# A hand-ordered RWKV-7 + SwiGLU kernel: the same 5742 steps in another order, with SyncE's transfers taken to land later

## The chip, the cores and the metric

The kernel runs on one core of a Trainium2 chip. The core has five engines that work at the same time, each through its own queue in order: TensorE (PE in the profile; PEld is its weight load), VectorE (DVE), ScalarE (ACT), GpSimd (POOL) and SyncE (SP), which here does nothing but start transfers. The metric is the device time of one execution in microseconds, of which several are timed; the median counts. A separate execution is profiled; it has a time of its own, and its span runs from the first to the last instruction.

## The reference, cut to what matters

```python
# r, k, v, w, a, b: (4, 8, 768, 40) float32, batch x heads x tokens x channels
for t in range(S):                                        # 768 tokens, one after the other
    y[:, :, t] = einsum('bhd,bhde->bhe', r_t, state)      # read the 40x40 state of each head
    Sa = einsum('bhde,bhe->bhd', state, a_t)
    state = state * w_t - outer(Sa, b_t) + outer(v_t, k_t)
x = y.transpose(0, 2, 1, 3).reshape(3072, 320)            # heads side by side
xn = x / sqrt(mean(x * x) + 1e-6) * rms_g
out = (silu(xn @ w_gate) * (xn @ w_val)) @ w_out          # 320 -> 1536 -> 320; inputs float64
```

There are 32 independent recurrences (4 batches, 8 heads), each over 768 tokens, and behind them a feed-forward block on 3072 tokens. The feed-forward inputs come as float64 and are made float32 on the chip.

## The kernel before, in words

Tokens are worked on in 24 chunks of 32. Within a chunk the recurrence is written as matrix products, and the part in which each token depends on the tokens before it becomes a unit triangular 32x32 matrix per recurrence, which has to be inverted. For every chunk `c` there are four pieces of program:

- `front(c)` loads the inputs w, a, k, b and v, turns them on PE (`turn`, L498), and builds decayed products over five levels (1, 2, 4, 8, 16 tokens). At each level PE makes 16 small products (`gram`, L495, written `ps<-A,KE`), DVE puts them under a mask into the tile `LT`, and ACT copies others into `KN`. When the last level is in `LT`, four transfers write it to DRAM (`sB<-LT`, L735) and four read it back in another layout into `M` (`M<-sB`, L742).
- `inverse(c)` is 31 pairs of DVE operations (`tmp`, `Yi`, L453) on `M`. Its result goes to DRAM by four transfers (`sY<-Yi`, L766) and comes back by four (`LT<-sY`, L768). The first four chunks use `early_inverse`, which inverts halves and joins them with two PE products (`ps<-M,LT` and `ps<-M`).
- `main(c)` uses the inverse: PE products `state` (`ps<-ST,aP`) and `lower` (`ps<-VU,LT`), an ACT scale `Xs`, the second `lower` (`ps<-Xs,LT`), which needs the inverse back in `LT`, four ACT copies into `VU`, then PE's `update` of the state and a `turn` of `VU`, an ACT copy `vut`, the `score` products, the five `level` products (`ps<-As,KN`), DVE sums into `y`, a `turn4` of `y`, the scaling by the root mean square, and a `turn3` into `xg`. Every second chunk it loads `rn` (r, two transfers of 160 KB).
- `feed(g)`, for two chunks together, is the feed-forward block: per pair of 128-wide slices PE does `h64`, `h` (`ps<-xg,w`) and `out` (`po<-w,hT`), ACT the silu (`sg`), DVE the product (`hT`); at the end four transfers write the result (`out_dram<-o`). `narrow` makes the float64 weights float32, 24 times, between the first chunks.

Chunks overlap: `front(c + 2)` and `inverse(c + 2)` run while `main(c)` does. The PE work of `feed` fills the gaps of the recurrences; it is the filler in this program.

The order is written out. `Plan` only records the 5742 steps with what each reads and writes. `ORDER`, a table of numbers, then says in which order they are issued: each number is a step's distance from the oldest step not yet issued. Each engine's queue is what ORDER leaves for that engine. A "-" in the table issues a filler matmul on the identity (L1010, `po<-ident`, 28 of them), which has no use but to keep PE busy. `PAIRS`, a second table, gives for each PSUM room which of three pairs of PSUM banks it takes (`ps0` to `ps2`); a room is free when its last reader has been issued and has run. All transfers but the first ones and the weights' and inputs' loads on POOL go through SP's queue, one behind the other: `sB`, `M`, `sY`, `LT`, `rn` and `out_dram`. A transfer that has to wait for its data holds up all behind it in that queue.

Of the kernel before, what the change touches and what calls it, by code (L numbers as in the profile page):

```python
# [33 lines left out]
363 362 58 54 55 60 59 56 6 5 391 44 46 28 133 4 39 7 8 40 72 53 10 196 364 367 9 368 68 57 365 193 27 11 13 366 185  # L34
188 184 74 73 69 75 373 12 14 15 369 388 380 70 189 16 17 18 66 183 71 81 80 372 79 84 389 83 42 - - 82 187 93 91 88 76
90 182 78 89 92 20 41 195 34 262 35 85 94 186 321 65 77 102 98 99 103 64 100 87 399 201 43 203 86 101 104 108 109 263
202 477 473 398 95 97 110 476 472 114 105 198 470 475 107 113 112 96 115 197 390 474 118 106 116 199 129 126 117 119
130 111 212 125 222 232 200 120 124 123 - 242 121 211 131 204 134 210 132 208 209 205 - 220 206 213 214 219 207 489 381
471 218 217 223 63 127 128 221 215 824 823 228 227 51 229 233 224 231 67 225 230 819 820 226 491 490 240 237 241 29 320
238 194 30 371 234 216 236 243 239 135 62 61 136 137 138 139 140 141 142 248 143 486 - - 244 235 144 145 247 146 147  # L40
488 382 259 246 148 149 258 249 150 245 151 152 153 154 155 156 36 21 370 254 253 487 260 255 0 156 157 158 159 160 161
251 162 163 835 491 1006 821 1002 338 1007 18 391 392 492 836 496 165 166 37 164 167 249 498 495 837 500 260 497 499
493 121 494 506 310 - 504 505 508 168 501 256 394 509 510 519 507 515 502 311 255 384 321 511 382 373 263 514 518 376
817 512 517 516 520 503 377 264 265 525 521 513 176 172 174 170 177 816 323 374 44 178 169 173 171 175 179 523 375 250
47 31 30 266 267 268 269 524 270 21 530 46 957 526 191 820 528 529 385 522 180 378 383 399 531 534 545 393 312 - 36 313
324 407 32 405 315 537 271 272 532 956 386 395 314 316 325 535 416 533 - 317 408 415 322 326 329 549 49 318 546 330 331
336 400 402 527 273 274 275 276 396 277 278 279 538 280 281 282 283 284 540 541 285 286 287 288 289 290 333 335 403 547
401 339 417 404 332 337 334 342 344 838 2 539 1 291 423 406 548 409 340 190 189 341 420 292 345 421 542 543 544 484 550
551 832 294 426 412 552 553 834 293 410 554 346 347 413 481 425 424 434 411 414 427 536 844 418 295 - 343 348 349 833
# [5 lines left out]
468 580 879 958 615 614 621 887 886 582 0 263 92 - - 261 93 267 259 517 525 602 266 603 604 0 647 538 290 94 316 267 95  # L55
# [10 lines left out]
765 770 79 0 221 572 14 0 381 382 16 761 570 359 - 77 576 - 383 281 17 579 0 370 566 752 106 750 0 0 427 63 0 203 204  # L66
205 213 366 564 367 562 565 559 570 563 558 63 59 207 746 102 104 211 427 60 368 569 288 429 1 3 0 62 759 564 367 368 0
367 759 569 571 368 570 369 580 370 576 208 202 205 758 564 371 259 57 563 260 0 371 567 2 0 371 - 59 208 60 204 202
259 0 207 0 0 569 368 206 207 61 996 274 277 62 369 575 370 371 372 373 374 375 376 420 422 421 424 584 561 423 275 256
0 0 375 376 377 378 379 380 381 382 577 569 570 578 55 0 55 254 0 0 - 380 381 382 383 568 577 384 420 422 423 421 0 0  # L70
559 574 561 529 266 578 0 575 559 584 423 582 55 382 428 426 51 425 583 383 - 578 568 384 385 386 581 387 429 388 389
52 595 570 390 594 424 56 0 524 390 426 568 0 578 577 390 1 0 983 0 2 - 425 427 416 987 986 0 581 0 414 0 384 385 587
# [970 lines left out]
```

## Time and profile before

| | us |
|---|---|
| median of 3 executions | 931.58 (930.19 to 933.2) |
| profiled execution, its own time | 934.37 |
| its span | 932.6 |
| PE busy in the span | 875.7 (94%) |
| DVE, ACT, POOL busy | 723.2, 521.9, 294.9 |
| mean granted TensorE clock by the profile | 0.991 |

A row of a group of instructions gives the line, engine, operation, names (written<-read), sizes, how many, then busy time and mean duration of one in nanoseconds, then the time the engine stood idle just before them and who ended it. A row of the timeline has start and duration, and in brackets the idle time before and its releaser. A row of waits names who waited for whom, with total time, number and longest. The row of a window has its length and then for each engine busy time and count, the granted clock of TensorE and the DMA engines' share.

### The profile page before, as it was taken

The page shows a single profiled execution, that of the slowest core. Times are in us where ns is not written, and L with a number is a line of the kernel's source. Part 1 is how long each engine was busy: PE and PEld are TensorE (multiplying, and loading weights), DVE is VectorE, ACT ScalarE, POOL GpSimd, SP SyncE. Part 2 cuts the span into 40 slices and gives each one's busy share as a digit, 9 for nine tenths or more (in the row PEclk, how much of TensorE's full clock was granted, in tenths as well). Part 3 has the DMA queues.
Part 4 walks back from the last instruction along what each step waited for, and adds up shares of the span by engine and source line. Part 5 has one row for each costly group of instructions (what it writes and reads, how often), then busy time and mean ns, then how long its engine had stood idle before and what let it go on. Part 6 is the DMA issues. An engine that isn't in the chain of part 4 may idle for free.

```text
span 932.6 us, 50195 instructions
## 1 busy us (share of the span) xinstructions
PE 875.7 (94%) x22072; PEld 703.2 (75%) x22072; DVE 723.2 (78%) x2702; ACT 521.9 (56%) x1144; POOL 294.9 (32%) x515
## 2 busy tenths in 40 slices
PE   4776898899999999999999999999999999999998
PEld 4665776677777788777777887887787777878776
DVE  5887778878878888978888888888888887864511
ACT  5887877674555566565555655655545454432211
POOL 8576546404221323432221333412503320200000
PEclk9999999899999999999999999999999999999999
DMA  9653546223242243333323223413414222021000
GB/s 162 104 119 84 126 98 153 73 69 67 55 87 49 46 86 73 71 59 60 70 39 74 64 54 75 89 35 71 88 21 85 61 41 62 11 60 28 3 15 15
DMA packets 146363, 63.01 MB, mean 68 GB/s; under 512 B 128800, under 2 KB 138080, under 8 KB 146144
## 3 DMA queue, kind: packets, MB, share of 16 engines
q1 hardware_dynamic: 125664, 29.46, 17.1%
q0 software_dynamic: 18368, 30.01, 15.1%
q8 instruction: 173, 2.83, 1.3%
q10 hardware_dynamic: 2112, 0.33, 0.3%
q14 instruction: 46, 0.38, 0.1%
HBM read 49.15 MB, written 10.09 MB: 64 GB/s over the span
## 4 chain that ended last, share of the span: by engine, by line
PE 72%; DMA 9%; DVE 6%; ACT 6%; issue 3%; SPq 2%; POOL 1%; DVEq 0%; POOLq 0%; ACTq 0%
PE ps L495 50%; PE po L495 14%; PE ps L498 7%; SPq L492 2%; DMA M<-sB 2%; DMA w<-in_moe_w_out_dram 1%; DMA LT<-sY 1%; DMA w<-in_moe_w_gate_dram 1%; DVE tmp L453 1%; DVE y L453 1%; DMA sY<-Yi 1%; ACT VU L476 1%; ACT KE L476 1%; DVE Yi L453 1%; DMA sY<-M 1%
## 5 line engine op out<-in xcount | busy, mean ns | idle before, releaser
L495 PE MATMUL ps<-xg,w 128*128 128x256 f32 (+1 forms) x1728 | 354.2, 393 | 1.2 <-DVE Yi L453 0.5
L495 PEld LDWEIGHTS ps<-xg,w 128*128 128x128 f32 (+1 forms) x1728 | 263.7, 191 | 49.1 <-issue 12.4
L495 PE MATMUL po<-w,hT 128*128 128x320 f32 x576 | 179.0, 449 | 0.0
L492 POOL DMA_DIRECT2D VU<-in_v_dram x184 | 102.4, 560 | 172.7 <-PE ps L495 78.1
L453 DVE TENSOR_TENSOR tmp<-Yi,M 128x60 f32<-128x60 f32 (+24 forms) x620 | 129.3, 209 | 20.5 <-DMA M<-sB 6.1
L453 DVE TENSOR_TENSOR Yi<-Yi,tmp 128x60 f32<-128x60 f32 (+24 forms) x620 | 129.7, 210 | 13.8
L473 ACT ACTIVATE sg<-ps 128x256 f32<-128x256 f32 x144 | 52.6, 384 | 150.6 <-PE ps L495 143.1
L495 PEld LDWEIGHTS po<-w,hT 128*128 128x128 f32 x576 | 106.0, 192 | 37.4 <-issue 1.9
L476 ACT COPY KE<-K 128x512 f32<-128x512 f32 x168 | 110.6, 662 | 26.2 <-DVE K L453 18.2
L453 DVE TENSOR_TENSOR hT<-ps,sg 128x256 f32<-128x256 f32 x144 | 58.3, 420 | 68.7 <-ACT sg L473 57.4
L453 DVE TENSOR_TENSOR K<-K,T 128x256 f32<-128x256 f32 x240 | 98.9, 421 | 10.2 <-ACT KE L476 8.8
L495 PE MATMUL ps<-A,KE 40*64 40x72 f32 x3840 | 95.0, 247 | 9.0 <-ACT KE L476 1.7
L495 PEld LDWEIGHTS ps<-A,KE 40*64 40x64 f32 x3840 | 79.2, 149 | 28.9 <-issue 9.3
L476 ACT COPY KN<-ps 128x320 f32<-128x320 f32 x144 | 67.4, 471 | 59.1 <-PE ps L495 28.5
L453 DVE COPY_PREDICATED LT<-msk,ps 128x256 f32<-128x256 uint32 x120 | 65.9, 550 | 19.5 <-PE ps L495 10.2
L482 POOL TENSOR_TENSOR ss<-ss,mhalf 128x1 f32<-128x1 f32 x24 | 15.4, 641 | 194.2 <-DVE ss L453 179.2
L453 DVE TENSOR_TENSOR y<-y,ps 128x256 f32<-128x256 f32 x119 | 49.9, 419 | 11.0 <-PE ps L495 7.9
L453 DVE TENSOR_TENSOR A<-A,T 128x128 f32<-128x128 f32 (+1 forms) x168 | 55.8, 335 | 1.5 <-ACT A L476 0.4
L495 PEld LDWEIGHTS ps<-As,KN 64*40 64x40 f32 x3840 | 45.1, 123 | 12.7 <-issue 4.4
L495 PE MATMUL ps<-As,KN 64*40 64x32 f32 x3840 | 50.3, 204 | 3.1 <-DVE y L453 1.6
L476 ACT COPY VU<-ps 32x320 f32<-32x320 f32 x96 | 40.0, 417 | 15.5 <-PE ps L495 14.2
L492 POOL DMA_DIRECT2D wan<-in_w_dram x44 | 29.1, 661 | 57.4 <-PE ps L498 57.1
(121 smaller groups left out, 1250.2 us busy)
## 6 DMA issues: line engine op xcount, KB each, us to landing
M<-sB SPq DMA_DIRECT2D x80, 128.0 KB, 3.4
rn<-in_r_dram SPq DMA_DIRECT2D x24, 160.0 KB, 4.6
out_dram<-o SPq DMA_DIRECT2D x48, 80.0 KB, 2.3
VU<-in_v_dram POOLq DMA_DIRECT2D x184, 20.0 KB, 2.6
kbn<-in_b_dram POOLq DMA_DIRECT2D x44, 80.0 KB, 3.4
kbn<-in_k_dram POOLq DMA_DIRECT2D x44, 80.0 KB, 3.3
wan<-in_w_dram POOLq DMA_DIRECT2D x44, 80.0 KB, 3.1
wan<-in_a_dram POOLq DMA_DIRECT2D x44, 80.0 KB, 3.3
```

Source lines behind the costliest of these rows:

```text
L453: plan.add("DVE", kind, lambda at: fn(at(o), *m(at)), [o], aps(*args))
L473: plan.add("ACT", "act", lambda at: nc.scalar.activation(at(o), at(a), f, **kw), [o] + aps(acc), [a])
L476: plan.add("ACT", "copy", lambda at: nc.scalar.copy(at(o), at(a)), [o], [a])
L482: plan.add("POOL", "tt", lambda at: nc.gpsimd.tensor_tensor(o, a, b, op), [o], [a, b])
L492: plan.add(by, "dma", lambda at: queue.dma_start(out=o, in_=i), [o], [i])
L495: return o, lhsT, rhs, lambda at: nc.tensor.matmul(at(o), lhsT, rhs, start=start, stop=stop, skip_group_check=True)
L498: return o, i, ident, lambda at: nc.tensor.transpose(at(o), i, ident)
```

## The change: another order

The operations are the same: the same 5742 steps with the same operands, and 28 filler matmuls. What differs is the two tables. ORDER was found anew by a planner that takes each transfer begun by SyncE to land later than its median; with it the pairs of PSUM banks and the places of the fillers were found anew.

```diff
 ORDER = """
-363 362 58 54 55 60 59 56 6 5 391 44 46 28 133 4 39 7 8 40 72 53 10 196 364 367 9 368 68 57 365 193 27 11 13 366 185
+5 4 6 8 7 9 10 11 12 13 14 15 16 17 18 27 363 373 391 362 39 40 54 59 60 55 28 56 381 364 133 194 42 380 72 73 74 58
...
 PAIRS = """
-20404040232242442445224024020000004244422202002424404224422422440012040400242420024244400242220004220404040400022442020
+20404020014242442423002400424420042022200020222004424004402200042010224404422002204040200424222420044442420204204002024
...
```

The engines' queues are alike in a few stretches: PE's order is the same from the `turn4` of chunk 1 to the middle of `feed(0)`, again for 25 steps in chunk 8, and for the last 144 of its steps, from chunk 20's end on. Elsewhere two of five PE steps have the same neighbour as before.

The first place is SP's queue at the inverse of chunk 11. `sY_176` is the DRAM buffer through which the inverse (`Yi`) goes back into `LT_104`; `rn` is the load of r, `out_dram` a piece of the output. Before:

```order
L492 DMA sY_176<-Yi_138 256x1x32
L492 DMA rn_97<-in_r_dram 64x16x40
L492 DMA sY_176<-Yi_138 256x1x32 x3
L492 DMA LT_104<-sY_176 32x8x32
L492 DMA out_dram<-o_170 32x2x320
L492 DMA LT_104<-sY_176 32x8x32 x3
L492 DMA rn_97<-in_r_dram 64x16x40
```

Now:

```order
L492 DMA M_135<-sB_173 32x1024 x2
L492 DMA sY_176<-Yi_138 256x1x32 x4
L492 DMA LT_104<-sY_176 32x8x32 x4
L492 DMA rn_97<-in_r_dram 64x16x40
L492 DMA out_dram<-o_170 32x2x320
```

The load of r and the piece of output stood between the transfers of the inverse, and now stand behind them.

The second place is PE's queue around the `turn4` of chunk 3 (`ident,y_147`). `As,KN` are the last three `level` products of that chunk, which DVE adds into `y_147`; `xg,w` is a filler from `feed(0)`. Before:

```order
L498 MATMUL ps_63<-ident,wan_95 104x64 x16
L495 MATMUL ps_64<-As_145,KN_0_105 40x32 x16
L495 MATMUL ps_64<-As_145,KN_0_108 40x32 x16
L495 MATMUL ps_64<-As_145,KN_0_111 40x32 x16
L495 MATMUL ps_65<-xg_152,w_164 128x256 x2
L495 MATMUL ps_65<-xg_152,w_165 128x256 x2
L495 MATMUL ps_65<-xg_152,w_164 128x256 x4
L495 MATMUL ps_64<-A_131,KE 64x72 x16
L498 MATMUL ps_63<-ident,y_147 128x40 x8
```

Now:

```order
L495 MATMUL ps_64<-As_145,KN_0_111 40x32 x16
L498 MATMUL ps_65<-ident,wan_95 104x64 x16
L495 MATMUL ps_64<-As_145,KN_0_108 40x32 x16
L495 MATMUL ps_64<-As_145,KN_0_105 40x32 x16
L495 MATMUL ps_63<-A_131,KE 64x72 x16
L498 MATMUL ps_64<-ident,y_147 128x40 x8
L495 MATMUL ps_65<-xg_152,w_164 128x256 x2
```

The feed-forward products that stood between the last level product and the turn now stand behind the turn.

The third place is the start of POOL's queue, which loads the first weights (`w_162`) that ACT makes float32 first. Before:

```order
L492 DMA w_162<-in_moe_w_out_dram 128x448
L509 ISA
L509 AFFINE_SELECT ident<-ident 128x128
L492 DMA w_162<-in_moe_w_gate_dram 128x2x256
L548 IOTA vut_91 128x32
```

Now:

```order
L548 IOTA vut_91 128x32
L488 MEMSET wan_95 128x16x24
L492 DMA w_162<-in_moe_w_out_dram 128x448
L492 DMA w_163<-in_moe_w_val_dram 64x256
L492 DMA w_165<-in_moe_w_val_dram 64x256
L492 DMA w_162<-in_moe_w_gate_dram 128x2x256
```

The load of the gate weights was POOL's second transfer and is now its fourth. On SP the first load of r (160 KB) has moved from the fifteenth transfer to the fifth, among the first inputs.

More of the change, by code (lines that the diff above doesn't have):

```diff
@@ L33 @@
 ORDER = """
-363 362 58 54 55 60 59 56 6 5 391 44 46 28 133 4 39 7 8 40 72 53 10 196 364 367 9 368 68 57 365 193 27 11 13 366 185
[L35 to L48, printed above, removed]
@@ L69 @@
[L69 to L72, printed above, removed]
[31 rows of a table removed]
+5 4 6 8 7 9 10 11 12 13 14 15 16 17 18 27 363 373 391 362 39 40 54 59 60 55 28 56 381 364 133 194 42 380 72 73 74 58
@@ new lines @@
+367 53 57 20 34 46 69 75 - 372 41 19 35 - 368 70 71 193 80 79 32 83 76 320 82 81 84 88 89 93 92 90 78 94 91 77 85 62
+184 189 188 185 201 187 95 100 87 365 47 99 49 101 98 102 476 190 262 103 86 202 104 109 108 203 110 105 113 112 96 114
+115 36 97 106 107 119 472 191 389 130 186 67 182 116 118 111 183 198 29 199 129 48 388 131 200 212 121 222 43 232 473
+66 475 477 120 211 242 63 204 210 117 - - 205 208 64 209 213 470 370 474 134 214 220 206 219 207 382 221 218 217 223
+231 215 132 229 227 228 233 224 225 230 489 226 216 65 237 238 241 240 234 235 243 248 247 125 123 126 124 128 127 135
@@ new lines @@
+136 137 239 - 244 490 491 383 138 139 245 321 258 366 68 140 141 196 471 142 252 143 486 - 144 145 249 236 488 259 246
+260 824 263 819 255 253 254 61 192 195 823 820 146 147 148 149 150 836 261 492 817 487 151 152 153 154 155 371 156 157
+158 159 160 161 162 163 164 165 493 311 166 496 250 500 497 494 390 838 498 499 509 501 837 374 495 375 505 385 510 506
+312 502 322 - 507 511 51 44 508 22 517 369 519 515 516 1003 503 377 339 376 521 504 45 384 23 512 514 167 168 392 818
+520 - 522 256 257 264 525 265 266 267 268 513 38 523 518 269 528 270 526 821 169 173 175 177 171 393 527 178 24 524 529
[5 rows of a table added]
@@ new lines @@
+843 295 844 848 429 420 296 855 841 26 852 431 432 853 297 0 433 297 49 841 414 421 855 599 481 1006 1019 601 853 848 -
[4 rows of a table added]
+555 443 444 935 937 424 858 425 594 593 595 556 862 863 592 872 426 596 598 857 600 601 602 603 607 333 604 608 - 0 275
+- 271 276 277 224 290 126 289 119 122 985 272 - 95 316 602 642 278 298 297 535 0 95 222 299 298 317 123 278 97 524 96 0
[5 rows of a table added]
+339 451 298 299 449 455 300 159 85 453 341 340 452 351 87 88 301 302 86 457 352 74 75 215 218 0 354 - 459 461 458 75 88
[3 rows of a table added]
+0 381 581 570 582 0 371 270 0 0 0 2 3 369 566 565 63 - 562 431 67 750 106 370 0 206 207 208 0 0 366 558 565 564 59 60
[4 rows of a table added]
@@ L104 @@
+568 560 575 559 577 573 - 47 578 569 383 582 579 584 384 420 385 386 581 595 570 580 - 423 431 594 425 424 589 588 387
+388 389 390 391 392 393 434 394 395 427 1 2 3 0 0 428 424 421 2 677 680 0 0 44 - 0 387 419 421 423 47 587 426 0 426 427
[3 rows of a table added]
+556 557 558 559 560 561 562 563 564 346 343 263 924 925 344 694 - 943 944 945 360 392 393 394 565 745 395 0 608 691 611
[27 rows of a table added]
 1014 675 452 1015 1162 1161 1006 849 848 853 854 852 455 445 1145 1146 1142 807 808 994 809 810 811 1003 855 1013 1010
@@ L107 @@
 1029 1167 459 1102 950 1405 1403 1406 947 1105 1104 460 - 1030 1031 1032 872 873 823 824 1164 1103 1168 1169 1033 461
[3 rows of a table removed]
-951 952 - 725 642 726 729 591 592 727 732 644 593 594 646 595 645 1096 734 643 596 649 651 730 0 651 646 596 597 730
-598 408 409 737 599 686 476 734 735 736 750 600 601 602 603 931 649 739 738 1 751 647 604 652 605 653 413 - 685 1138
[26 rows of a table removed]
-1152 1015 1016 1017 1018 862 943 944 1393 685 1019 1161 1162 436 440 1020 817 818 3 820 1165 1175 1185 - 430 1153 1163
[3 rows of a table removed]
-1179 1196 1100 1041 1194 1093 - 439 1187 1101 1192 1042 1178 1197 1189 1199 1104 1043 1044 1045 1046 1047 1188 1198
[8 rows of a table removed]
@@ L152 @@
-423 981 973 835 979 790 985 791 974 977 - 418 - 982 419 984 840 792 424 420 986 983 793 841 794 664 991 665 795 666 988
-842 796 845 797 1142 944 1140 1138 1135 667 798 426 668 987 1141 681 989 843 427 992 844 799 800 801 993 802 803 804
-996 805 806 807 808 809 810 811 848 846 847 994 1096 1139 1097 1099 669 849 1098 412 431 416 995 1008 1003 1000 1002
-1001 855 856 854 1085 1137 850 851 852 812 428 1012 429 1009 432 853 813 814 999 433 1010 1151 1004 1011 1153 857 - 421
[15 rows of a table removed]
-1141 943 939 801 849 992 994 984 850 802 851 993 3 1 - 416 852 853 803 1136 686 1008 1009 838 839 1154 1010 804 1155
[26 rows of a table removed]
@@ L198 @@
-952 954 953 613 966 758 754 1147 755 759 760 752 976 - 0 827 828 610 611 612 613 954 955 641 830 615 616 957 757 758
[36 rows of a table removed]
[11 rows of a table added]
+972 783 - 980 - 415 835 973 981 987 428 988 1093 432 784 984 985 982 836 833 834 785 420 638 679 684 941 683 434 786
[6 rows of a table added]
+- 838 1166 1194 450 1157 1173 446 1175 822 823 821 442 1040 1179 1180 1041 1185 1171 1158 820 1042 1172 1086 1167 1182
[16 rows of a table added]
+820 819 821 0 738 726 747 597 751 653 - 1123 655 16 752 0 734 756 593 744 594 730 652 595 596 651 649 745 597 598 599
[10 rows of a table added]
+806 849 668 669 1009 1008 938 944 1139 807 808 427 431 1002 809 852 810 811 812 813 814 853 670 428 671 1010 - 1011 432
[10 rows of a table added]
@@ new lines @@
+1077 0 2 673 417 674 - 957 959 958 692 7 3 418 419 420 968 967 4 624 970 8 971 972 421 977 760 759 758 626 757 765 969
[6 rows of a table added]
+1151 1153 1152 1157 802 803 998 804 1161 805 1165 425 - 863 426 806 1000 1158 864 431 427 807 1162 808 865 942 1397
+1399 866 1166 1160 997 867 432 868 1163 1094 809 1001 1002 1007 1005 810 811 812 813 814 815 816 428 669 1164 1159 1171
+1170 433 - 1083 429 1006 1004 1084 1167 1086 1169 1096 1176 1098 1175 1173 1013 435 1014 1015 1016 1168 1185 1195 838
[20 rows of a table added]
+427 704 665 666 670 669 668 0 227 663 228 604 605 606 607 608 609 610 424 743 1 734 735 740 744 746 749 736 - 6 747 748
[39 rows of a table added]
@@ L235 @@
 """
 PAIRS = """
-20404040232242442445224024020000004244422202002424404224422422440012040400242420024244400242220004220404040400022442020
-42002244244004442200202220420424242444424040440022204040424404444204404404202224220200004042042224442242242042022020020
-44420420240004202040424222444000202000402000044204000020024242244444440440004002422220420200402242224244042242422420400
-04444244402202242422424040024422404224424242204220004424020402200024220442020400444024242000442422224242444004004420200
@@ L242 @@
-42220044024200200400200442020422400000444420204
+20404020014242442423002400424420042022200020222004424004402200042010224404422002204040200424222420044442420204204002024
+42440444420020202044022242200242202342040440024000400444040020444004202400224420424222220204000004042420002202420402222
+20442004040244200202442420404400240204402404402000040444402042244420004444220444024242022222044022020420240440400204024
+24200242424024220220004044400204044404444244424022222002002022024200420002040002002042424020424222400024422020024200400
@@ L243 @@
+24440020240420200200402024242044022222000042420
 """
```

5 lines of the change are left out of this document (removed), and 332 rows, old and new, of the table ORDER.

## The prediction

> **What bounds the kernel now.** I read the page's busy line first, then the windows by stage, then PE's waits and its timeline, and last SP's queue at the stalls.
>
> ```profile
> span 932.6 us, 50195 instructions
> PE 875.7 (94%) x22072; PEld 703.2 (75%) x22072; DVE 723.2 (78%) x2702; ACT 521.9 (56%) x1144; POOL 294.9 (32%) x515
> ```
>
> PE idles 932.6 - 875.7 = 56.9 us in all. The same work in another order can win at most that, and what a lowered clock costs. Where the idle time lies, the windows show (length, then busy time of PE, PEld, DVE, ACT and POOL, granted clock, share of the DMA engines, GB/s):
>
> ```profile
> 0.00:25.00 25.00, 12.68 (x230) 10.63 (x230) 14.43 (x44) 14.69 (x27) 19.66 (x49) 1.00 0.98 158
> 25.00:108.00 83.00, 60.28 (x1876) 52.56 (x1878) 68.56 (x234) 68.40 (x141) 50.41 (x91) 1.00 0.55 112
> 108.00:140.00 32.00, 30.68 (x740) 24.60 (x740) 25.22 (x73) 26.10 (x57) 17.20 (x30) 1.00 0.43 91
> 140.00:178.00 38.00, 32.88 (x980) 25.57 (x977) 32.51 (x116) 27.00 (x56) 20.40 (x34) 1.00 0.51 115
> 178.00:188.30 10.30, 9.84 (x167) 7.62 (x156) 8.64 (x29) 6.83 (x15) 6.68 (x12) 0.50 0.38 87
> 188.30:313.00 124.70, 119.43 (x3199) 95.18 (x3197) 101.75 (x395) 72.24 (x166) 31.91 (x54) 0.99 0.32 64
> 340.00:460.00 120.00, 116.59 (x3309) 92.40 (x3301) 103.48 (x407) 69.25 (x157) 37.84 (x63) 0.99 0.37 69
> 460.00:780.00 320.00, 317.39 (x8320) 254.50 (x8309) 271.68 (x1049) 175.46 (x387) 89.65 (x150) 1.00 0.31 61
> 780.00:932.60 152.60, 148.97 (x2567) 118.27 (x2566) 72.61 (x262) 45.48 (x108) 9.29 (x17) 1.00 0.11 24
> ```
>
> Up to 108 us PE idles 35.0 us: there chunk after chunk has to come through DVE and ACT, and no feed-forward work is at hand. From 108 to 313 us it idles 12.2, from 340 to 460 us 3.4, from 460 to 780 us 2.6. Past 140 us PE is the bound, so a PE stall taken away there is time won. From 780 us the order is unchanged.
>
> The clock matters as much. In 178 to 188.3 us it was at half, and the profile's clock column hides more:
>
> ```profile
> L495 PE MATMUL ps<-A,KE 40*64 40x72 f32 x276 | 10.7, 330 | 2.1 <-ACT KN L476 1.5 <-ACT A L476 0.5
> L495 PE MATMUL ps<-A,KE 40*64 40x72 f32 x224 | 4.9, 228 | 0.0
> 406.70:410.10 3.40, 1.84 (x71) 1.10 (x71) 3.30 (x14) 0.41 (x1) 2.39 (x4) 1.00 1.19 180
> 410.10:413.50 3.40, 3.40 (x26) 2.06 (x28) 0.07 (x1) 2.83 (x7) 0.00 (x0) 0.51 0.18 17
> ```
>
> The first two rows are the same product in 30 to 60 us and in 350 to 400 us: 330 ns against 228, so the start ran at a low clock although the windows say 1.00 there. The last two say that a window of 3.4 us in which PE was busy 1.84 was followed by one at half clock.
>
> Where PE stalls past 140 us, in its timeline (the brackets hold the idle time before):
>
> ```profile
> 156.96 0.73 PE L495 MATMUL ps<-A,KE 40*64 40x72 f32 x32 [1.61 <-ACT T L476]
> 169.12 0.72 PE L495 MATMUL ps<-M 16*32 16x16 f32 x64 [0.90 <-ACT M L476]
> 242.62 0.79 PE L495 MATMUL ps<-Xs,LT 32*32 32x40 f32 x64 [0.95 <-ACT K L476]
> 281.35 0.79 PE L495 MATMUL ps<-Xs,LT 32*32 32x40 f32 x64 [1.13 <-ACT r L476]
> 408.92 1.15 PE L495 MATMUL ps<-Xs,LT 32*32 32x40 f32 x64 [1.43 <-issue]
> 449.46 0.78 PE L495 MATMUL ps<-Xs,LT 32*32 32x40 f32 x64 [1.23 <-DMA LT<-sY]
> ```
>
> Four of the six stand before the second `lower` of chunks 5, 6, 10 and 11, which needs the inverse back from DRAM. What SP did before the last two (timeline of SP, and two rows of the chain of waits):
>
> ```profile
> 396.80 1.22 SPq L492 DMA_DIRECT2D sY<-Yi  x2
> 398.06 0.60 SPq L492 DMA_DIRECT2D out_dram<-o  x1
> 398.70 1.21 SPq L492 DMA_DIRECT2D sY<-Yi  x2
> 403.68 5.59 DMA LT<-sY
> ...
> 436.86 0.63 SPq L492 DMA_DIRECT2D rn<-in_r_dram  x1
> 443.33 0.34 SPq L492 DMA_DIRECT2D out_dram<-o  x1
> 443.72 1.52 SPq L492 DMA_DIRECT2D LT<-sY  x3
> 444.79 4.54 DMA LT<-sY
> ...
> LT<-sY SPq DMA_DIRECT2D x80, 32.0 KB, 3.0
> ```
>
> The median from issue to landing is 3.0 us (last row, DMA issues); here the last transfer took 5.59 and 4.54, with an output piece or a load of r issued among the eight. This is just what a planner that counts on the median gets wrong.
>
> **The change, part by part.** *The two stalls on the inverse's return.* I counted, along DVE's and PE's own orders with the mean duration of each kind of row, how far the last `Yi` operation and the second `lower` moved. In 14 of the chunks 4 to 20 the distance grows, in 3 it shrinks (chunk 4 by 1.6 us, 7 by 1.3, 18 by 2.0); the mean is +1.3. At chunk 10 it grows by 3.5 us against a stall of 1.43. At chunk 11 it grows by 0.5, and `rn` and `out_dram` leave the eight transfers (0.63 + 0.34), together 1.5 against 1.23. Both go: -2.7 us, bounds 0 and -2.7.
>
> *The clock behind the first of them.* Without the 1.43 us the window 406.7 to 410.1 is as busy as its neighbours and the next 3.4 us run at full clock. By the product above that is worth at least 3.4 x (1 - 228/330) = 1.05 us, by the clock itself at most 1.7; I take -1.4, bounds 0 and -1.7. [...]
>
> *The stalls at 242.6 and 281.4 us.* ACT copies ended these (`K`, `r`), which free the PSUM pair that `lower` takes. Their distances grow by 1.2 and 2.1 us, but the pairs are dealt anew, so half: -1.0, bounds 0 and -2.1. *Those at 157.0 and 169.1* end on ACT as well. Between the turn of w and a and its `gram` PE has 0.3 us less other work than before, so the first stays. Between the two `inv` products it has 1.1 us more, so the second goes: -0.9 for both, bounds 0 and -2.5.
>
> *New waits.* Chunk 4 loses 1.6 us of distance but also two `M<-sB` issues among its eight transfers. Chunks 14, 15 and 16 get 3, 5 and 1 foreign issues of about 0.6 us, against +4.4, +3.2 and +2.6 us. I put 0.3 on the three shrunken places. Two new ones are on PE:
>
> ```profile
> L453 DVE TENSOR_TENSOR y<-y,ps 128x256 f32<-128x256 f32 x119 | 49.9, 419 | 11.0 <-PE ps L495 7.9 <-ACT y L476 0.9
> L476 ACT COPY vut<-ps 128x1024 f32<-128x1024 f32 x24 | 24.3, 1011 | 9.9 <-PE ps L498 9.7
> L495 PE MATMUL ps<-As,KN 64*40 64x32 f32 x320 | 3.9, 200 | 0.0
> ```
>
> At chunk 3's `turn4` DVE has five `y` operations left after the `level` product of length 4, 5 x 0.42 = 2.1 us. PE now does two more level products (3.9/10 = 0.39 us each), a turn and a `gram` (4.9/7 = 0.7 us) meanwhile, about 1.9 us. With hand-overs some 0.6 us are missing, all six operations if DVE comes late. At chunk 2's `score` only a half-microsecond stands against the 1.01 us `vut` copy: 0.6. New waits in all +1.5, bounds 0 and +4. DVE's own waits for `M<-sB` are off PE's path past 140 us, where `h` and `out` keep PE fed: 0; without that cover, up to 2.6 each.
>
> *The start.* ACT's first conversion waits for the gate weights and stands ahead of the first `K` copies (chain, ACT's timeline, PE's waits):
>
> ```profile
> 2.46 6.13 DMA w<-in_moe_w_gate_dram
> 8.71 0.72 ACT L473 ACTIVATE ex<-w,ctop 128x480 f32<-128x480 int16 x1 [5.21 <-DMA w<-in_moe_w_gate_dram]
> 10.84 1.07 ACT L476 COPY K<-ps 128x512 f32<-128x512 f32 x2
> PE ps L498 <- DMA kbn<-in_b_dram: 9.6, 1, 9.6
> ```
>
> As POOL's fourth transfer it is issued some 2 us later (a memset and two more issues of about 0.56 us, with what else moved ahead). It lands near 10.6, and `K` starts near 11.3 instead of 10.84. The early 160 KB of r come on top of DMA engines 98% busy, for up to 1.6 us by their packets. Against that, two more conversions stood ahead of `T` and `A`, and are now behind. I take +0.5. Bounds: +2.3 (0.7 for the later landing, 1.6 for r), and -2.5, for which a tenth of the 22.7 us that PE idles between 25 and 108 us would have to go.
>
> Sum: -2.7 - 1.4 - 1.0 - 0.9 + 1.5 + 0.5 = -4.0 us. Against the profiled execution's own 934.37 us (its span and 1.8 us around it) that is 930.4. That execution is 2.8 us above the median of the runs, 931.58, from which the forecast is **927.6 us**.
>
> **The rivals.** *Nothing won (no change).* The distances grow for transfers, but PE then waits on ACT and PSUM, as two of the four `lower` stalls already did; 460 to 780 us, where only 2.6 us are idle, can give nothing. Wins and new waits cancel: about 931. Against it: the two largest late stalls are plainly transfers.
>
> *Slower: the clock falls at chunk 3.* If the `turn4` of chunk 3 and the waits near it idle PE for about 1.4 us within 3.4 us, the clock halves there. At 178 us it stayed low for 10.3 us, which cost up to half, 5.1 us. If that comes on top of the old one, the wait itself is 2 us (the six `y` operations late), and 931.6 - 4.0 + 5.1 + 2.0 = 934.7. For it: two places of the new order are tight there. Against it: much of the neighbouring idle time goes. It decides from a gap of 1.4 us on.
>
> *Faster still.* The stalls around 169 to 179 us thin out, and the half clock at 178 us goes: -4.0 - 5.1 gives about 922.5. For it: more work lies ahead of `inv`. Against it: the `turn` of `VU` in chunk 3 moves nearer to its copies.
>
> *The change doesn't do what it says.* The distances show that it does; only chunk 11's gain in distance is thin.
>
> **How the numbers follow.** A measurement of this kernel tells about 0.3% (2.8 us) from no change. Forecast 0.36 (927.6), faster still 0.12 (922.5), no change 0.29 (931), slower 0.23 (934.7). So faster 0.48, within 0.3% 0.29, slower 0.23. The range goes from 920 (every stall named, the clock at 410 us and the better start: -2.7 - 1.7 - 2.1 - 2.5 - 2.5 = -11.5) to 935 (the slower rival). The forecast's own range is 923 to 929.
>
> **What would show it.** Right: no half clock at the second `lower` of chunk 10, no PE stall over 0.5 us ended by `LT<-sY`, PE idle past 140 us down from 21 us to some 16. Wrong: PE idles as long as before with other releasers; a stretch of half clock at chunks 2 to 4; chunk 1's `turn4` later than 107.8 us by more than 1 us, which the unchanged order behind it would carry to the end.

## The result: slower, by something the prediction had not priced

| | before | after |
|---|---|---|
| median of 6 executions, us | 932.39 (928.91 to 934.17) | 946.27 (941.69 to 949.75) |
| profiled execution, its own time | 934.37 | 946.13 |
| span | 932.6 | 944.1 |
| PE busy, PE idle in the span | 875.7, 56.9 | 881.0, 63.1 |

The ratio is 1.0156, with a 95% interval of 1.012 to 1.0191. The forecast was 927.6 us in a range of 920 to 935, with slower as the least likely sign at 0.23. It was wrong in sign and in size.

The windows by stage tell where. Both orders meet at a few places, where the same products stand on either side: at the last turn of chunk 1, at the start of chunk 8, and from 780 us on in the kernel before. So each kernel is cut at its own times for these places, and at 540 us. Columns are the length of the window, then busy time of PE, PEld, DVE, ACT and POOL, the granted clock, the DMA engines' share and GB/s. Before:

```profile
0.00:107.80 107.80, 72.77 (x2102) 62.98 (x2103) 82.79 (x276) 83.09 (x167) 70.07 (x139) 1.00 0.65 123
107.80:366.60 258.80, 246.43 (x6621) 196.37 (x6621) 217.04 (x803) 165.20 (x364) 96.69 (x161) 0.97 0.37 78
366.60:540.00 173.40, 169.65 (x4568) 134.52 (x4568) 149.20 (x592) 98.35 (x217) 49.93 (x83) 0.99 0.32 62
540.00:784.10 244.10, 241.99 (x6388) 194.27 (x6388) 205.12 (x790) 131.43 (x293) 68.87 (x115) 1.00 0.32 63
784.10:932.60 148.50, 144.88 (x2408) 115.11 (x2402) 69.08 (x244) 43.86 (x104) 9.29 (x17) 1.00 0.11 23
```

After:

```profile
0.00:110.20 110.20, 73.44 (x2104) 63.10 (x2104) 85.20 (x276) 83.76 (x167) 71.04 (x139) 1.00 0.60 121
110.20:367.90 257.70, 245.66 (x6619) 194.35 (x6618) 217.02 (x803) 164.65 (x364) 96.31 (x160) 0.97 0.36 77
367.90:540.00 172.10, 170.88 (x4659) 136.56 (x4661) 153.70 (x606) 99.48 (x217) 52.19 (x88) 1.00 0.35 68
540.00:795.50 255.50, 246.10 (x6318) 195.25 (x6306) 202.46 (x769) 130.14 (x293) 66.42 (x112) 0.98 0.28 58
795.50:944.10 148.60, 144.96 (x2408) 115.28 (x2404) 70.26 (x253) 43.80 (x104) 9.35 (x17) 1.00 0.11 23
```

Length less PE's busy time gives PE's idle time: 35.0, 12.4, 3.75, 2.1 and 3.6 us before, 36.8, 12.0, 1.2, 9.4 and 3.6 after. The start lost 1.7, the stretch up to 540 us won 2.5 as predicted, and the stretch behind it, of which the prediction said that it "can give nothing", lost 7.3. The clock went the same way: full from 366 to 540 us after the change, and below full from 540 on, where it had been full.

The 7.3 us are two stalls for the most part, each before the second `lower` of a chunk (15 and 20), each with a half clock beside it: at chunk 15 it begins at 577.5 us, inside the stall, at chunk 20 at 768.7, right behind it. PE's timeline after the change, two windows of rows:

```profile
575.48 0.42 PE L498 MATMUL ps<-ident,y 40*128 40x40 f32 x8
578.76 0.49 PE L495 MATMUL ps<-Xs,LT 32*32 32x40 f32 x16 [2.86 <-issue]
...
764.25 1.08 PE L495 MATMUL ps<-xg,w 64*128 64x256 f32 x8
768.20 0.94 PE L495 MATMUL ps<-Xs,LT 32*32 32x40 f32 x64 [2.88 <-DVE hT L453]
```

and the windows of 3.4 us around them:

```profile
574.10:577.50 3.40, 1.80 (x29) 1.30 (x27) 3.12 (x17) 0.91 (x3) 0.00 (x0) 1.00 0.00 0
577.50:580.90 3.40, 2.14 (x66) 1.89 (x67) 1.71 (x8) 0.79 (x2) 1.77 (x3) 0.51 0.17 33
580.90:584.40 3.50, 3.50 (x7) 1.79 (x6) 0.00 (x0) 1.99 (x5) 0.00 (x0) 0.50 0.01 1
...
765.30:768.70 3.40, 0.53 (x56) 0.50 (x57) 2.71 (x10) 1.80 (x3) 0.00 (x0) 1.00 0.00 0
768.70:772.10 3.40, 3.40 (x39) 2.77 (x26) 0.00 (x0) 2.84 (x7) 0.00 (x0) 0.50 0.02 5
```

Stalls of 2.86 and 2.88 us and some 10.2 us at half clock (granted 0.50 and 0.51 in these windows), which by that clock cost up to half of it, make 10.8 of the 11.5 us by which the span grew. (The eight `po<-w,hT` products from 577.6 to 584.3 us took 754 ns each, against 443 ns from 590 to 640 us. The other terms nearly cancel: start and smaller stalls against the gain up to 540 us.)

Neither stall is a transfer. In the first, the inverse's return had been issued long before. SP's timeline, and the tile's answer for 560 to 580 us with its landing times (min, median, max):

```profile
569.93 1.80 SPq L492 DMA_DIRECT2D LT<-sY  x4
...
DMA to landing us min/median/max: 1.7/1.8/3.1
```

The last of the four was issued at 571.3 us and so had landed by 574.4, 4.4 us before the product that needs it. At chunk 20 the four were issued from 756.56 to 759.55 us, and no landing of the tile took longer than 3.7 us there, so the operand lay ready by 763.3, 4.9 us early. What ended 0.1 us before that product is a DVE instruction, the second `hT` here (DVE's timeline, with an ACT row above it that gives the `sg` it reads):

```profile
575.16 0.38 ACT L473 ACTIVATE sg<-ps 128x256 f32<-128x256 f32 x1 [2.04 <-PE ps L495]
...
575.61 0.21 DVE L453 TENSOR_TENSOR Yi<-Yi,tmp 128x48 f32<-128x48 f32 x1
575.85 0.23 DVE L453 TENSOR_TENSOR tmp<-Yi,M 128x69 f32<-128x69 f32 x1
...
577.45 0.41 DVE L453 TENSOR_TENSOR hT<-ps,sg 128x256 f32<-128x256 f32 x1
577.78 0.21 DVE L453 TENSOR_TENSOR tmp<-Yi,M 128x60 f32<-128x60 f32 x1
577.90 0.42 DVE L453 TENSOR_TENSOR K<-K,T 128x256 f32<-128x256 f32 x1
578.24 0.41 DVE L453 TENSOR_TENSOR hT<-ps,sg 128x256 f32<-128x256 f32 x1
```

`hT` is the last reader of the PSUM pair that the second `lower` takes, and the program makes the product wait for it: the `lower` of chunk 15 holds a wait for just this second `hT`, and that of chunk 20 for the second `hT` there. Its `sg` was there at 575.54. It stood in DVE's queue until 578.24, behind inversion steps of the next chunk and a few others, and DVE had no gap. At chunk 20 it is the same, with 15 other steps of several kinds around the two `hT`; the second one ended at 768.15, 0.05 us before the product:

```profile
767.73 0.42 DVE L453 TENSOR_TENSOR hT<-ps,sg 128x256 f32<-128x256 f32 x1
```

The theory to test, called A: **the loss is an instruction that frees a PSUM pair and stands late in its engine's queue, and the half clock beside that wait.** Its rivals: B, it is a matter of where the stalls fall against the clock's windows, so that any shift moves the loss; C, the product waits for its transfer, or DVE is simply full, so that the order of DVE's queue is nothing.

### The profile page after: what moved, and what is told of

The parts are those of the page before. It is cut to its first block, busy times and chain, and to the rows that moved or that the text cites. A ratio compares the mean times of both kernels' runs of the same rounds, so it can differ in the third digit from the quotient of the medians.

```text
span 944.1 us, 50196 instructions
## 1 busy us (share of the span) xinstructions
PE 881.0 (93%) x22072; PEld 704.5 (75%) x22072; DVE 728.6 (77%) x2702; ACT 521.8 (55%) x1144; POOL 295.3 (31%) x515
## 3 DMA queue, kind: packets, MB, share of 16 engines
q0 software_dynamic: 18368, 30.01, 14.6%
## 5 line engine op out<-in xcount | busy, mean ns | idle before, releaser
L495 PE MATMUL po<-w,hT 128*128 128x320 f32 x576 | 182.4, 454 | 0.0
L495 PE MATMUL ps<-A,KE 40*64 40x72 f32 x3840 | 94.5, 246 | 10.3 <-ACT KE L476 4.3
L476 ACT COPY KN<-ps 128x320 f32<-128x320 f32 (+1 forms) x144 | 66.6, 470 | 64.9 <-PE ps L495 25.1
L495 PE MATMUL ps<-As,KN 64*40 64x32 f32 x3840 | 52.8, 205 | 4.7 <-DVE y L453 2.6
L492 POOL DMA_DIRECT2D kbn<-in_b_dram x44 | 29.0, 660 | 83.4 <-PE ps L498 83.4
```

Source lines behind the costliest of these rows:

```text
L476: plan.add("ACT", "copy", lambda at: nc.scalar.copy(at(o), at(a)), [o], [a])
L492: plan.add(by, "dma", lambda at: queue.dma_start(out=o, in_=i), [o], [i])
L495: return o, lhsT, rhs, lambda at: nc.tensor.matmul(at(o), lhsT, rhs, start=start, stop=stop, skip_group_check=True)
```

## The experiments

Each run is compared with the kernel before, run on the same chip beside it. Its median there was 933.06 us for e1 to e4, 935.68 for e5 to e8 and 932.51 for e9 and e10. The changed kernel itself was not run again beside them, so a run is set against it by the two ratios to the kernel before.

### Which stretch: the two orders spliced

At the meeting places the two orders can be cut and joined. Three kernels take one stretch from the change, the rest from before (the pairs 0 and 2 change names at the first cut).

```diff
 # ORDER and PAIRS, by the count of steps issued
-1..5742 as before
+e1: 1..760 as after, 761..5742 as before
+e2: 1..760 as before, 761..2050 as after, 2051..5742 as before
+e3: 1..2050 as before, 2051..5742 as after
```

> The changed kernel's order and pairs for the first 760 operations (up to about 107 us, where both orders meet at the last turn of chunk 1), the kernel before's from there on. In the profiles that turn ran 2.3 us later after the change than before. Theory A (the loss lies after 560 us, in products that wait for a PSUM pair which VectorE frees late, and in the half clock behind those waits; the start costs 2 us more, the middle gives about 1 back): 932.4 + 2.3 = about 934.5 us. Theory B (the loss is set by where the stalls fall against the clock's 3.41 us windows, so that any shift of the start moves the half-clock stretches everywhere): the stretches at 178, 274 and 410 us of the kernel before vanish or move, and the time departs from 934.5 by more than 3 us either way.

> The changed kernel's order only between the two meeting points (operations 760 to 2050, about 107 to 314 us, chunks 2 to 7 with their fronts), the kernel before's on both sides. In the profiles the changed kernel made up 1.3 us in this stretch. Theory A: 932.4 - 1.3 = about 931 us, with a stall of near 2.9 us at a turn of front 6 (166 us) kept. Theory B: the half-clock stretches at 134, 168 and 192 us of the changed kernel do not come back, since the start is 2 us earlier, and the time falls to 926 or less.

> The kernel before's order up to the meeting point at about 314 us (operation 2050), the changed kernel's from there. In the profiles the changed kernel gained up to 5 us between 340 and 545 us and lost 15.5 us between 545 and 780. Theory A: 932.4 + 10.5 = about 943 us, with stalls of near 2.9 us at the second lower product of chunks 15 and 20, each waiting for a PSUM pair that VectorE's hT frees 0.1 us earlier, and a half clock of 3.4 to 6.8 us beside each. Theory B: the stalls stay, the half clock beside them does not, and the time is 938 us or less.

Measured: 934.79 us for the start (ratio 1.0012, 0.9987 to 1.0037), 934.02 for the middle (1.0007, 0.9984 to 1.003), 944.75 for the late part (1.0127, 1.0089 to 1.0165). The late part carries the loss, and the other two can't be told from no change. The start came out as theory A has it, within the interval of no change, and the middle 3 us above. In e3 the stalls at chunks 15 and 20 were there again, 2.92 and 2.87 us, with 10.2 us of half clock behind 540 us, though everything ahead of them ran otherwise. Of theory B one thing is true: the half clock between 108 and 314 us is not a property of the order. In e3 that stretch is the kernel before's, step by step, and the clock was at half there for 20.5 us against 13.7 in the kernel before's own profile.

### The suspected cause taken away

Four `hT` move up in DVE's queue and nothing else. Rows of DVE's order at chunk 15 and at chunk 20 (`Yi_137` and `Yi_138` are the inverses of chunks 16 and 21):

```diff
 TENSOR_TENSOR T_127<-T_127 128x32
+TENSOR_TENSOR hT_168<-ps_65,sg_166 128x256
+TENSOR_TENSOR hT_168<-ps_65,sg_166 128x256
 TENSOR_TENSOR Yi_137<-Yi_137,tmp_140 128x2x24
 ...
 TENSOR_SCALAR ss_148<-ss_148 128x1
-TENSOR_TENSOR hT_168<-ps_65,sg_166 128x256
 TENSOR_TENSOR tmp_140<-Yi_137,M_135 128x60
 TENSOR_TENSOR K_129<-K_129,T_127 128x64x4
-TENSOR_TENSOR hT_168<-ps_65,sg_166 128x256
 ...
 TENSOR_TENSOR Yi_138<-Yi_138,tmp_140 128x3x21
+TENSOR_TENSOR hT_168<-ps_65,sg_166 128x256
 TENSOR_TENSOR A_131<-A_132,T_126 128x8x8x2
 ...
```

> The changed kernel with four VectorE instructions moved up in their queue and nothing else: the two hT products ahead of the second lower of chunk 15 go ahead of nine steps of the inversion, the two ahead of the second lower of chunk 20 ahead of 16 mixed steps. Theory A: both stalls go (2.86 and 2.88 us, of which the first keeps up to 0.8) and with them the half-clock stretches beside them (6.8 and 3.4 us at half speed, 5.1 us of lost work): 946.3 - 5 - 5 = about 936 us. Theory C (the lower products wait for the landing of their operand from memory, or VectorE is full there whatever its order): the stalls stay within 0.5 us of their length, now ended by the transfer or by another VectorE product, and the time stays at 945 to 947.

Measured: 935.1 us, ratio to the kernel before 1.0026 (1.0003 to 1.0048), against 1.0156 with the change as it was. Four instructions of 0.42 us in another place are worth about 12 us. PE's timeline of this run at the two places:

```profile
575.57 0.42 PE L498 MATMUL ps<-ident,y 40*128 40x40 f32 x8
576.52 0.78 PE L495 MATMUL ps<-Xs,LT 32*32 32x40 f32 x64 [0.53 <-issue]
...
760.56 0.79 PE L495 MATMUL ps<-Xs,LT 32*32 32x40 f32 x64
```

and its windows from 368.3 us on, as above:

```profile
368.30:540.00 171.70, 170.52 (x4621) 136.21 (x4621) 153.35 (x605) 99.40 (x217) 52.10 (x87) 1.00 0.36 69
540.00:786.30 246.30, 242.36 (x6344) 193.13 (x6340) 202.96 (x770) 130.17 (x293) 66.40 (x112) 1.00 0.29 59
```

The second stall is gone, the first is 0.53 us, idle time behind 540 us falls from 9.4 to 3.9, and the clock is full there. Theory C falls: the operand was there, and DVE had the time.

One of the two places alone, the first:

```diff
 # DVE's order at chunk 20, against e4; chunk 15 as in e4
-TENSOR_TENSOR hT_168<-ps_65,sg_166 128x256
 TENSOR_TENSOR A_131<-A_132,T_126 128x8x8x2
 ...
 TENSOR_TENSOR T_126<-T_126 128x64
+TENSOR_TENSOR hT_168<-ps_65,sg_166 128x256
```

> The changed kernel with only the two hT products ahead of chunk 15's second lower moved up. Theory A: the stall of 2.86 us at 579 us shrinks to at most 0.8 and its half clock of 6.8 us goes, 2.1 + 3.4 = 5.5 us less; the stall of 2.88 us at chunk 20 and its half clock stay. About 13.9 - 5.5 = 8.4 us above before, 1.009. Theory B (the stalls matter only through the clock's windows, so moving everything behind by 5 us changes what the second one costs): the half clock at chunk 20 goes too or doubles, 1.007 or 1.011.

Measured: 940.78 us, ratio 1.0087 (1.0054 to 1.012). The stall at chunk 15 shrank to 0.54 us, without a half clock, and that at chunk 20 stayed, with its half clock of 3.4 us:

```profile
761.93 0.88 PE L495 MATMUL ps<-Xs,LT 32*32 32x40 f32 x64 [2.87 <-DVE hT L453]
```

So the first place is worth about 0.7%, and the second, by e4, about 0.6%.

### The cause put into the kernel before

If a late `hT` is enough, one can be made late where nothing else was changed. At chunk 20 of the kernel before, the `hT` that frees the pair of the second `lower` moves down by ten instructions:

```diff
 TENSOR_TENSOR tmp_140<-Yi_138,M_136 128x63
-TENSOR_TENSOR hT_168<-ps_64,sg_166 128x256
 TENSOR_TENSOR Yi_138<-Yi_138,tmp_140 128x3x21
 ...
 COPY_PREDICATED LT_103<-msk,ps_65 128x64x4
+TENSOR_TENSOR hT_168<-ps_64,sg_166 128x256
 TENSOR_TENSOR xg_153<-ps_65,gcol 128x3x128
```

> The kernel before with one VectorE instruction moved down: the hT product that frees the PSUM pair of chunk 20's second lower goes behind ten other VectorE instructions, to about 760.1 us instead of 757.24. Theory A (such a product late in VectorE's queue is enough to make the loss): a stall of about 2.3 us before that lower, and in most executions a half clock of 3.4 us behind it, 1.7 us more: 933 + 2.3 + 1.7 = about 937 us. Theory C (the pair would be waited for by nobody, since other products of TensorE are at hand, or the loss needs the transfers of the changed kernel): time within 1 us of before.

Measured: 939.93 us, ratio 1.0046 (1.0021 to 1.007), so 4.2 us slower. PE's timeline:

```profile
755.51 1.23 PE L495 MATMUL ps<-A,KE 40*64 40x72 f32 x64
759.29 0.79 PE L495 MATMUL ps<-Xs,LT 32*32 32x40 f32 x64 [2.55 <-DVE hT L453]
```

The stall is 2.55 us. In this profiled execution, whose own time of 936.25 us is the lowest of the ten, the clock stayed full behind it (its mean is 0.991, as in the kernel before's own profile). That the others are slower because of the clock is likely by the sizes, but not shown: they have no profile. So a late `hT` alone makes the stall; how often the half clock comes with it is open.

### Was the stall that the prediction took for a transfer one?

The same reading puts a question to the prediction. In the kernel before, the product at 408.92 us also starts 0.1 us behind an `hT` (end 408.82), and that `hT` had waited in DVE's queue for 2.9 us:

```profile
408.40 0.42 DVE L453 TENSOR_TENSOR hT<-ps,sg 128x256 f32<-128x256 f32 x1
```

The prediction had read that stall as the landing of `LT<-sY`. In this run the `hT` goes ahead of seven others (the expectation counts eight):

```diff
 TENSOR_TENSOR Yi_138<-Yi_138,tmp_139 128x3x20
+TENSOR_TENSOR hT_168<-ps_65,sg_166 128x256
 COPY_PREDICATED LT_102<-msk,ps_64 128x256
 ...
 TENSOR_TENSOR T_125<-T_125 128x32
-TENSOR_TENSOR hT_168<-ps_65,sg_166 128x256
```

> The kernel before with one VectorE instruction moved up: the hT product that frees, at 408.82 us, the PSUM pair of chunk 10's second lower (start 408.92, after 1.43 us idle) goes ahead of eight others, to about 406.2 us. The prediction put that stall down to the landing of LT<-sY. If the landing bounds it (the last of its four transfers near 409.3 us): the lower ends when it did, within 0.3 us, and the half clock behind it stays in most executions; time within 1 us of before. If the pair bounds it: the idle time goes, the half clock at 410 us with it, 1.4 + 1.7 = 3 us, about 930.

Measured: 935.84 us, ratio 0.9999 (0.9973 to 1.0026). PE's timeline:

```profile
407.90 1.34 PE L495 MATMUL po<-w,hT 128*128 128x320 f32 x4
409.18 0.26 PE L495 MATMUL ps<-Xs,LT 32*32 32x40 f32 x4
410.14 0.25 PE L495 MATMUL ps<-Xs,LT 32*32 32x40 f32 x2 [0.70 <-DMA LT<-sY]
410.87 0.76 PE L495 MATMUL ps<-Xs,LT 32*32 32x40 f32 x58 [0.48 <-DMA LT<-sY]
```

The product now begins without a stall and then waits twice inside, for the transfer. It ends at 411.63 us in an execution that was 1.8 us late already, against 410.07 in the kernel before. Pair and landing were both late there, the landing by a little more: the pair set when the product began, the landing when it ended, and in that the prediction's reading holds. The expectation that the half clock stays behind it is not borne out by this execution, which has none there and one of 3.4 us from 430 us, at another product. A row's bracket names one of two late releasers, or `issue`, and which of them bounds is only told by moving one.

### The start

SyncE's first 160 KB of r go behind ten other transfers, and two more `hT` (chunks 17 and 18) move up:

```diff
 DMA wan_95<-in_w_dram 32x16x40 x2
-DMA rn_97<-in_r_dram 64x16x40
 DMA VU_98<-in_v_dram 32x4x40
 ...
 DMA wan_95<-in_a_dram 32x16x40
+DMA rn_97<-in_r_dram 64x16x40
```

> The changed kernel with SyncE's first 160 KB of r issued after the second VU and two wan transfers instead of fifth, and with six hT products moved up on VectorE (the four of the run before, and one each ahead of the second lower of chunks 17 and 18). Theory A on the start (the four early transfers of r and the wide weight loads hold up the last of kbn, so that the first product starts at 11.56 instead of 9.63 us): first product near 10 us, 1.5 us earlier; the waits at 647 and 682 us shrink from 0.95 and 0.90 to at most 0.5 each. 935.1 - 1.5 - 1.3 = about 932 us. Rival (the first product waits for the weight loads on the other queue, not for r): first product stays within 0.4 us of 11.56, time about 934.

Measured: 934.62 us, ratio 0.9992 (0.9968 to 1.0016). The first product starts at 10.20 us:

```profile
10.20 1.10 PE L498 MATMUL ps<-ident,kbn 64*104 64x64 f32 x16 [10.20 <-DMA kbn<-in_b_dram]
```

It was 11.56 after the change and 9.63 before. So r's place in SP's queue holds 1.4 of the 1.9 us. The stall at chunk 17 is gone, that of chunk 18 is 0.42 us.

### Can the order win?

First the late part alone, with the six `hT` moved:

```diff
+1..2050 as before, 2051..5742 as after, hT moved at chunks 15, 17, 18 and 20
```

> The kernel before's order up to 314 us, the changed kernel's from there, with the six hT products moved up. Theory A: the changed order's gain of 2.7 us idle and 1.7 us of half clock between 340 and 540 us is kept and its loss behind 545 us is gone but for about 1 us: 933 - 4.4 + 1 = about 929.5 us, a ratio near 0.996. Rival (without the late stalls the order has nothing to give, the work between 340 and 540 was only moved): 933 to 935.

Measured: 935.82 us, ratio 1.0008 (0.9983 to 1.0033): no gain, as the expectation's rival had it. PE idles 1.4 us less behind 371 us than in the kernel before, but 24 us behind the seam a stall stands that neither of the two kernels has, with a half clock of 3.4 us behind it:

```profile
336.34 0.60 PE L498 MATMUL ps<-ident,ST 40*104 40x40 f32 x16
338.68 0.44 PE L498 MATMUL ps<-ident,y 40*128 40x40 f32 x8 [1.74 <-DVE tmp L453]
```

So the second version keeps the changed order from chunk 1 on, and moves three copies up on ACT as well, each of which freed a pair late there (`KN` of front 5, `y` of chunk 3, `r` of chunk 6):

```diff
 # ACT, the first of the three places
 ACTIVATE o_170<-w_165,ctop 128x480
+COPY KN_2_107<-ps_65 128x320
 ACTIVATE o_170<-o_170,cmid 128x480
 ACTIVATE o_170<-o_170 128x480
 ...
 ACTIVATE sg_167<-ps_63 128x256
-COPY KN_2_107<-ps_65 128x320
```

> The kernel before's start (760 operations), the changed kernel's order behind it, with the six hT products moved up on VectorE and three copies moved up on ScalarE: KN of front 5 ahead of two weight conversions (TensorE waited 2.42 us for its PSUM pair at 164 us), y of chunk 3 ahead of a weight conversion that waited for a landing (1.1 us idle at 190 us), the second r of chunk 6 ahead of rE (0.89 us at 277 us). Theory A (what costs is the copy or product that frees a PSUM pair and stands late in its engine's queue): 4.4 us of idle go, the 4.4 us that the changed order gains between 340 and 540 us stay, 1 us is lost behind 545: 8 us less than before, 0.991, or 6 us if the seam at 107 us costs what it did in the run with two seams. Rival (such waits come back elsewhere, as TensorE is full): within 3 us of before.

Measured: 930.77 us (927.25 to 932.34, 12 executions) against 932.51 for the kernel before, ratio 0.9982 (0.9961 to 1.0002). It has the lowest ratio of all kernels here, 1.7% under the changed one's, but that it beats the kernel before is not shown; and the gain is 1.7 us where 6 to 8 were expected. Its windows:

```profile
108.70:363.60 254.90, 244.62 (x6616) 194.51 (x6616) 216.61 (x803) 164.85 (x364) 96.03 (x160) 0.98 0.37 78
363.60:540.00 176.40, 174.81 (x4755) 139.34 (x4756) 157.02 (x618) 101.47 (x223) 52.20 (x88) 1.00 0.35 68
540.00:781.10 241.10, 238.37 (x6204) 190.15 (x6202) 199.36 (x757) 128.04 (x288) 66.39 (x112) 1.00 0.30 60
```

PE idles 10.3, 1.6 and 2.7 us in these, 14.6 in all against 18.2 in the kernel before: 3.6 us won, where 4.4 + 2.7 - 1 = 6.1 were expected. The wait that the moved `KN` was to remove had 2.42 us in e5 (2.89 in the changed kernel). Of it 0.6 is still there, and 0.8 stands at the next `turn`, for an `hT`:

```profile
161.57 0.64 PE L498 MATMUL ps<-ident,kbn 64*104 64x64 f32 x12 [0.61 <-ACT sg L473]
...
175.68 0.66 PE L498 MATMUL ps<-ident,VU 64*104 64x64 f32 x16 [0.81 <-DVE hT L453]
```

In that part the expectation's rival was right: where PE is nearly full (busy 244.6 of 254.9 us), a wait taken away was in part waited for at the next place. Why PE's busy time did not fall with the shorter half clock (876.2 us against 875.7) is open.

## Why the prediction was wrong, step by step

- *The two stalls on the inverse's return, -2.7.* Right. PE's idle time from 366 to 540 us fell by 2.5. Of PE's waits the first row is the kernel before's, the second the changed one's:

```profile
PE ps L495 <- DMA LT<-sY: 1.4, 2, 1.2
```

```profile
PE ps L495 <- DMA LT<-sY: 0.2, 1, 0.2
```

  e7 shows that the end of the product at chunk 10 was bounded by the landing as the prediction said, though by a narrow margin over a late pair that it had not seen.
- *The clock behind the first, -1.4.* Right in sign: after the change the clock was full from 366 to 540 us. Whether it came differed between executions: the same stall (1.44 us in e1, 1.45 in e2) had half clock behind it in e1 and none in e2 (last section). The length of a gap alone does not tell it in these runs: half clock came with gaps of 2.86 and 2.88 us in the changed kernel and 1.44 us in e1, and none with 2.55 us in e6.
- *The stalls at 157, 169, 242.6 and 281.4, -1.9.* The first two and the one at 242.6 are gone, that of chunk 6 stayed at 0.88 us, and a new one of 2.89 came at 165.7, on ACT's `KN`. From 108 to 367 us PE idles 0.3 less. Each stall was argued by itself, and the new neighbours were not.
- *New waits, +1.5 with bounds 0 and +4.* **This is the step that failed.** For the chunks behind 460 us the prediction counted distances for transfers only: from the last `Yi` to the second `lower`, and the foreign issues among the eight transfers. That part held where the trace was read for it: at chunk 15, with five foreign issues, the operand was there 4.4 us early. The prediction knew that a `lower` also needs a free PSUM pair, from the stalls at 242.6 and 281.4 us, and named such waits in a rival. But it gave no price to where the new order puts the instruction that frees the pair in another engine's queue. Two stalls of 2.86 and 2.88 us came of it, and 10.2 us at half clock, up to 10.8 us where the term had +1.5 and at most +4. Taking four `hT` out of their late places (e4) took back 5.5 of the 7.3 us of idle time behind 540 us and all the half clock there.
- *"460 to 780 us ... can give nothing."* True for a gain. It was read as if nothing could be lost there either, and the slower rival was therefore put at chunk 3, which did not decide anything: from 108 to 367 us the half clock was 13.7 us before and after. The gap of 1.4 us from which that rival was to decide was an estimate from one stall, the 1.43 us at 408.92; behind the 1.61 us at 156.96 the clock stayed full up to 178.0, though PE was busy only 1.80 us from 154.15 to 157.56. A stretch in which PE hardly waits (2.1 us idle out of 244) has as much to lose as any other, as e6 shows, where one `hT` ten places later makes a stall of 2.55 us.
- *The start, +0.5 with bounds -2.5 and +2.3.* The sign was right, the size was at the upper bound: the first product is 1.9 us later, and the last turn of chunk 1 some 2.4 (110.2 us against 107.8). In the median e1 can't tell that from no change. The prediction named the 160 KB of r and priced them at up to 1.6; e5 gives 1.4 for them. Its other term, the conversions ahead of `K`, was not on the path: the last of the `kbn` landed too late.
- *DVE's waits for `M<-sB`, 0.* Right: those before `tmp` fell from 6.1 to 1.2 us (DVE's groups by line), and PE had no use of it.
- *What would show it.* No half clock at chunk 10's `lower` and no stall over 0.5 us ended by `LT<-sY`: both came. PE idle past 140 us was to fall from 21 to 16 us; it rose to 25.2. "PE idles as long as before with other releasers" was listed as what would make the prediction wrong. It is what happened. So did its two other signs, chunk 1's `turn4` late by more than 1 us and half clock at chunks 2 to 4 (three stretches between 134 and 195 us), but e1 and e2 show that these did not make the loss.

Why the planner put those `hT` late is argued, not shown: a plan that takes the return to land later takes the second `lower` to start later too, and to that plan a late pair costs nothing. No run here touches the planner.

## What to carry to other kernels

When a re-ordered program is to be priced, ask of each product on the bound engine for everything that it needs: the operand, the buffer it writes, and for the buffer the instruction that frees it and how many stand ahead of that one in its own queue. A stretch with hardly any idle time (2.1 us of 244 here) had next to nothing to give, but much to lose: a stall of 2.5 to 2.9 us there cost 4 to 6 us here (e6, e4 and e10), more than its own length. Where a bracket names one releaser, or only `issue`, move the suspected instruction by itself before believing it: here four such moves won about 12 us and another, which looked alike, nothing.

## What was not expected of the hardware

Half clock came in steps of 3.41 us. Up to the last 2 us of the span it was 10.24, 3.41 and 3.41 us in the kernel before (from 178.0, 273.6 and 410.1 us), and 6.83, 3.41, 3.41, 6.83 and 3.41 after the change (from 133.8, 167.9, 191.8, 577.5 and 768.7). In each of the two executions these beginnings lie whole steps apart: 28 and 40 before, 10, 7, 113 and 56 after. The grid is not the same in all executions: e10's stretch from 18.4 us, below, begins 46.8 steps ahead of 178.0. What lowers the clock for a step is open. The same stall at chunk 10 was followed by half clock in e1 and not in e2, with the same busy time of PE in the window around it:

```profile
406.50:409.90 3.40, 1.96 (x84) 1.51 (x83) 2.89 (x12) 1.22 (x3) 1.91 (x4) 1.00 1.16 161
409.90:413.30 3.40, 3.40 (x52) 2.22 (x54) 0.25 (x1) 2.65 (x7) 0.00 (x0) 0.50 0.07 11
```

```profile
407.10:410.50 3.40, 1.95 (x72) 1.31 (x68) 3.30 (x14) 0.75 (x3) 2.85 (x5) 1.00 1.19 158
410.50:413.90 3.40, 3.20 (x98) 2.30 (x89) 1.10 (x5) 3.17 (x8) 0.00 (x0) 1.00 0.51 73
```

The first two rows are e1's windows, the last two e2's.

The prediction's reading that the start ran at a low clock, though the windows say 1.00 there, is borne out by e10. The record of the clock begins at 117 us in the profiles of the kernel before and of the changed one, and a window ahead of the record reads 1.00. In e10 it begins at 15 us, and it shows half clock from 18.4 to 117.4 us, with the `gram` products of 30 to 60 us at the same 324 ns (median) as in the kernel before. So a mean granted clock says little of an execution without a profile, as part of it depends on where the record begins (0.938 in e10, 0.991 in the kernel before).

And ACT's `sg` is made to wait for DVE's `hT` of the other half of the same PSUM pair, though of that pair both only read. The rows are the changed kernel's: an `sg` at chunk 20, and the sum of the waits of ACT's `KN` copies, which share nothing but the pair with the `LT` instructions that they wait for (an `sg` and an `hT` also share the tile `sg`):

```profile
765.77 0.38 ACT L473 ACTIVATE sg<-ps 128x256 f32<-128x256 f32 x1 [2.29 <-DVE hT L453]
...
ACT KN L476 <- DVE LT L453: 16.6, 17, 3.4
```

This `sg` had its product from PE at 757.5 us, so one late `hT` made the other one late too.
